# The first batch's expert guessed from v's column sums, and its A formed in two parts, in an attention and mixture-of-experts kernel

## The chip, the cores and the metric

The kernel runs on one core of one Trainium2 chip, in one launch. The metric is the device time of an execution in microseconds (us); before the change the median of 3 runs is 491.9 us (491.01 to 492.18). Short names of the engines: PE multiplies matrices (its weight loads are shown apart, as PEld), DVE, ACT and POOL work element by element, and SP issues most of the DMAs.

## The reference, cut to what matters

Two layers follow each other. The first is a Nystrom attention over 8 batches, 8 heads, 576 tokens and 64 values per head, with 32 landmarks (means over 18 tokens); the second is a sticky mixture of 8 experts over the 512 joined values of a token.

```python
A  = softmax(q @ k_lm.T)      # 576 x 32, one row for each token
Bm = softmax(q_lm @ k_lm.T)   # 32 x 32
C  = softmax(q_lm @ k.T)      # 32 x 576
Z  = Bm.T / (norm_1(Bm) * norm_inf(Bm) + 1e-6)
for _ in range(6):
    Z = 2 * Z - Z @ Bm @ Z
x = A @ Z @ C @ v
...
logits = x @ w_gate
for s in range(S):            # e is sticky along the tokens of a batch
    fresh_e = argmax(logits[b, s])
    e = fresh_e if s == 0 or local_gate[b, s] < 0.5 else prev_e
    out[b, s] = p[e] * (relu(x[b, s] @ w1[e]) @ w2[e])
```

The factors q and k are drawn eight times as large as v; v, w_gate, w1 and w2 are as drawn.

## The kernel before, in words

**One expert for a batch.** All tokens of a batch are sent through one expert, the one that most tokens choose (`votes`, L513). Tokens with another expert are gathered at the end into slots of 128 tokens, one expert and batch to a slot; the code runs one slot always and loops over `whole_slot` for any further ones.

**From attention to the expert.** x is not formed. The chain C, v and the six Newton steps on Z ends in a small matrix `wt` (`newton_w`, L419); `w_w1` (L608) multiplies it with the expert's w1 to G, which is cut into two float32r parts gh and gl; A, transposed, is cut into `ath` and `atl` (`a_split`, L489). `mm1` (L660) multiplies G with A for one chunk of 128 of the 1024 hidden values, with three products (gh with ath, gh with atl, gl with ath); the relu is taken on ACT and DVE (h, hx). The second product (L719, and L713 for the last 64 tokens) multiplies h with w2, also in two parts: wh is cut on ACT (L652), wl is formed on POOL (L657). A batch takes two passes of 8 chunks: first tokens 256 to 575, then tokens 0 to 255 (`PASSES`, L41). So the first pass of a batch needs 320 of its 576 columns of A, and the second pass the rest.

**What sets the order.** The attention of batches 1 to 7 is laid into the expert's chunks of the batches ahead of it: `SECOND` (L1122) and `PLANS` (L1127) hold for each step a time in chunks, at which it is written into the program; `G_AT`, `LATER` and `SLOT_AT` do the same for G, for the later part of the choice and for the slots. Over the first chunks `line_up` keeps all engines to the order as written. The first batch has nothing to hide behind: `first_attention` (L925) writes it by hand, ahead of all chunks. There the votes come last: A, `gate_weights`, `gates` and `votes` give the expert (L527), SP reads it from `regs` (L598), and only then its queue can issue the loads of w1 and w2 (L605, L647), for their address depends on it. `keep_warm` (L157) issues products of zeros, 11 at the start, 8 and 6 later on.

**DMA queues.** SP's queue is in order: an issue that waits holds those behind it. The loads of q and k have two buffers each, of v one.

## Time and profile before

| what | value |
|---|---|
| median of 3 runs | 491.9 us (491.01 to 492.18) |
| the profiled execution | 490.35 us, of which 488.6 us are the profile's span |
| PE busy in the span | 461.4 us (94%) |
| first product of the first chunk (L669) starts | 38.56 us |
| chunk 4 of the first batch starts | 54.56 us |
| second batch's first chunk starts | 103.60 us |
| the slot's expert ends, about | 480 us |
| granted PE clock | half (0.50, 1.2 GHz) from about 23 to 43 us, full (2.4 GHz) otherwise up to the end of the slot |

Times in the rows count from the span's start. A row of a timeline holds the start, the length, the engine, the line, the operation and its tiles (out<-in), and the count of instructions that are merged in it; in square brackets stands how long the engine idled before, and what it waited for. A matmul's length includes its way through the array, so that matmuls overlap: their pitch is the difference of starts.

### The profile page before, as it was taken

The page shows a single profiled execution, that of the slowest core. Times are in us where ns is not written, and L with a number is a line of the kernel's source. Part 1 is how long each engine was busy: PE and PEld are TensorE (multiplying, and loading weights), DVE is VectorE, ACT ScalarE, POOL GpSimd, SP SyncE. Part 2 cuts the span into 40 slices and gives each one's busy share as a digit, 9 for nine tenths or more (in the row PEclk, how much of TensorE's full clock was granted, in tenths as well). Part 3 has the DMA queues.
Part 4 walks back from the last instruction along what each step waited for, and adds up shares of the span by engine and source line. Part 5 has one row for each costly group of instructions (what it writes and reads, how often), then busy time and mean ns, then how long its engine had stood idle before and what let it go on. Part 6 is the DMA issues. An engine that isn't in the chain of part 4 may idle for free. (4 is left out here: it accounts for less than half of the span.)

```text
span 488.6 us, 12068 instructions
## 1 busy us (share of the span) xinstructions
PE 461.4 (94%) x4667; PEld 337.9 (69%) x4669; DVE 269.6 (55%) x807; ACT 210.7 (43%) x554; POOL 234.2 (48%) x355
## 2 busy tenths in 40 slices
...
GB/s 305 394 224 253 26 210 145 283 276 194 8 227 325 232 7 199 358 167 132 257 193 170 61 78 274 153 67 70 259 105 29 152 214 54 48 314 36 64 129 22
DMA packets 38701, 82.01 MB, mean 168 GB/s; under 512 B 3259, under 2 KB 4539, under 8 KB 37872
## 3 DMA queue, kind: packets, MB, share of 16 engines
...
q14 instruction: 23, 0.19, 0.1%
...
## 5 line engine op out<-in xcount | busy, mean ns | idle before, releaser
L719 PE MATMUL py<-wh,h 128*128 128x512 f32 x528 | 170.8, 405 | 1.7 <-ACT h L678 1.0
L657 POOL TENSOR_TENSOR wl<-raw,wh 128x512 fp32r<-128x512 f32 x72 | 92.5, 1303 | 91.2 <-ACT wh L652 80.5
L719 PEld LDWEIGHTS py<-wh,h 128*128 128x128 f32 x528 | 94.0, 188 | 31.1 <-issue 8.7
L678 ACT ACTIVATE h<-ph 128x256 fp32r<-128x256 f32 (+2 forms) x136 | 54.3, 403 | 124.5 <-PE ph L669 105.0
L681 DVE SCALAR_TENSOR_TENSOR h<-ph,h 128x256 fp32r<-128x256 f32 (+1 forms) x136 | 55.3, 409 | 76.7 <-ACT h L678 74.7
L719 PE MATMUL py<-wl,h 128*128 128x512 f32 x264 | 88.7, 394 | 0.0
L669 PE MATMUL ph<-ath,gh 128*128 128x320 f32 (+1 forms) x256 | 79.9, 312 | 1.6 <-DVE hx L684 0.8
L669 PE MATMUL ph<-atl,gh 128*128 128x320 f32 (+1 forms) x256 | 76.5, 299 | 0.0
L669 PE MATMUL ph<-ath,gl 128*128 128x320 f32 (+1 forms) x256 | 76.0, 297 | 0.0
L669 PEld LDWEIGHTS ph<-ath,gh 128*128 128x128 f32 x256 | 48.5, 189 | 17.5 <-issue 6.3
L719 PEld LDWEIGHTS py<-wl,h 128*128 128x128 f32 x264 | 49.5, 188 | 10.7 <-issue 0.5
L669 PEld LDWEIGHTS ph<-atl,gh 128*128 128x128 f32 x256 | 48.7, 190 | 4.1 <-issue 0.5
L669 PEld LDWEIGHTS ph<-ath,gl 128*128 128x128 f32 x256 | 48.6, 190 | 0.5 <-issue 0.5
L652 ACT CAST wh<-raw 128x512 fp32r<-128x512 f32 x72 | 43.1, 631 | 4.0 <-DMA raw<-w 3.9
L640 DVE TENSOR_TENSOR gl<-ph,gh 128x512 fp32r<-128x512 f32 (+1 forms) x19 | 12.5, 662 | 34.8 <-ACT gh L639 34.8
L734 ACT ACTIVATE ys<-py,pall 128x512 f32<-128x512 f32 x32 | 21.0, 689 | 15.6 <-DMA out<-ys 10.1
L639 ACT CAST gh<-ph 128x512 fp32r<-128x512 f32 (+1 forms) x19 | 10.6, 565 | 37.7 <-PE pg L626 26.4
L221 POOL TENSOR_TENSOR t<-q_t 128x288 f32<-128x288 f32 x28 | 21.3, 784 | 5.7 <-DVE regs L527 2.9
L221 POOL TENSOR_TENSOR t<-k_t 128x288 f32<-128x288 f32 x24 | 18.6, 794 | 8.6 <-DMA k_t<-kT 4.1
L713 PE MATMUL pg<-wh,h 128*128 128x512 f32 x56 | 22.4, 400 | 0.0
L713 PE MATMUL pg<-wl,h 128*128 128x512 f32 x56 | 22.3, 398 | 0.0
L626 PE MATMUL ph<-raw,wt 64*32 64x512 f32 (+1 forms) x136 | 19.7, 604 | 2.5 <-DMA raw<-w 2.5
(314 smaller groups left out, 719.8 us busy)
## 6 DMA issues: line engine op xcount, KB each, us to landing
...
raw<-w SPq DMA_DIRECT2D x17, 1024.0 KB, 7.2
v_t<-v SPq DMA_DIRECT2D x8, 1024.0 KB, 6.7
...
q_t<-qT SPq DMA_DIRECT2D x6, 1152.0 KB, 5.7
k_t<-kT SPq DMA_DIRECT2D x6, 1152.0 KB, 9.3
...
```

Of the source, the lines that this page charges most:

```text
L221: add = nc.gpsimd.tensor_add(t9[:, i], src[:, a + i, :, 0:9], src[:, a + i, :, 9:18])
L626: mm = nc.tensor.matmul(ps[g][32 * c:32 * c + 32, 0:n * P], w, w1[r, n * i:n * i + n, a * P:a * P + P], start=True, stop=True)
L639: st["cut"] = nc.scalar.copy(out=gh[:, g, x], in_=ps[g][:, 0:n * P]).ins.name
L640: last = nc.vector.tensor_tensor(out=gl[:, g, x], in0=ps[g][:, 0:n * P], in1=gh[:, g, x].bitcast(F32), op=ALU.subtract)
L652: cut = nc.scalar.copy(out=wh, in_=raw)
L657: nc.gpsimd.tensor_tensor(out=wl, in0=raw, in1=wh.bitcast(F32), op=ALU.subtract)
L669: mm = nc.tensor.matmul(hp, w[:, g, c], x[:, g, s0:s0 + n], start=(i == 0), stop=(i == 5))
L678: nc.scalar.activation(out=h[:, 0:e], in_=hp[:, 0:e], func=AF.Relu)
L681: nc.vector.scalar_tensor_tensor(out=h[:, 384:384 + m], in0=hp[:, 0:m], scalar=0.0, in1=h[:, 0:m].bitcast(F32), op0=ALU.max, op1=ALU.subtract)
L713: nc.tensor.matmul(yps[4], hs[ff][1], w, start=(ff == 0 and w is w2[ff][0]), stop=(ff == NC2 - 1 and w is w2[ff][1]))
L719: nc.tensor.matmul(yps[k], h[:, part + i * P:part + i * P + P], w, start=(f == 0 and part == 0 and w is wh), stop=(f == NC2 - 1 and part = ...
L734: nc.scalar.mul(out=ys, in_=yp, mul=st["pw"][:, k:k + 1])
```

## The change

The first batch's expert is no longer the result of its votes. Four things change in `first_attention`:

1. **A guess.** `guess_sums` sums v over the tokens for each of its 512 columns (20 products of 128-column weights, the upper halves of v as bfloat16, with a column of ones); `guess_scores` multiplies the sums with w_gate (8 products); `guess` takes the largest. The loads of w1 and w2 follow at once (`first_weights`), ahead of v, q and k of later batches on SP's queue. `votes` stops, for the first batch, ahead of its own matmul; tokens that choose another expert than the guessed one would go to the slots, as in any batch.
2. **A in two parts.** `a_scores`, `a_turn`, `a_max0`, `a_exp0`, `a_norm0` and `a_back0` take a part: tokens 256 to 575 ahead of the first chunk, tokens 0 to 255 as steps rs, rm, re, rn and rb among the chunks, at the times of `FIRST`. `gate_weights`, `gates`, the rest of the votes and the choice move there too.
3. **Newton steps with one addition,** for all batches: the two halves of the result are formed by one DVE addition (one of them with a block of zeros) in place of an ACT copy and a DVE addition.
4. **The start's order.** C's scores go ahead of B's, the second half of k of batch 0 comes in two DMAs, the landmarks of batch 1 go behind the first chunks, the fillers are 15 in place of 11, 8 and 6, PSUM banks are named for each use.

The tables `SECOND`, `PLANS`, `G_AT` and `SLOT_AT` have new times, most moved by up to one chunk, some by three; batch 1's second half of w1 and its w2 load at new times (`w1b`, `W2_AT`).

**SP, the loads around the first expert** (q_t, k_t, v_t: q, k, v; `regs`: the chosen expert; raw: w1 and w2; wtd: a store of wt). Before:

```order
L200 DMA q_t<-qT 128x1152
L201 DMA k_t<-kT 128x2x576
L200 DMA q_t<-qT 128x2304
L201 DMA k_t<-kT 128x4x576
L208 DMA v_t<-v 128x4x512
L209 DMA v_t<-v 64x512
L445 DMA wtd<-wt 128x128
L598 TENSOR_LOAD regs
L605 ISA
L605 DMA raw_539<-w 128x2x512
```

Now:

```order
L215 DMA q_t<-qT 128x1152
L217 DMA k_t<-kT 128x2x576
L663 TENSOR_LOAD regs
L670 ISA
L670 DMA raw_377<-w 128x2x512
```

The read of the expert stood behind batch 2's q and k (128x2304), batch 1's v and the store of wt; it now stands right behind batch 1's q and k.

**SP, further on, now** (raw_393 and raw_395 are w2 tiles 4 and 5 of the first batch, raw_572 is tile 6):

```order
L224 DMA v_t<-v 128x4x512
L225 DMA v_t<-v 64x512
L469 DMA wtd<-wt 128x128
L714 ISA
L714 DMA raw_393<-w 128x512
L714 ISA
L714 DMA raw_395<-w 128x512
L215 DMA q_t<-qT 128x2304
L217 DMA k_t<-kT 128x4x576
L714 ISA
L714 DMA raw_572<-w 128x512
```

Batch 1's v, the store of wt and batch 2's q and k stand among the first batch's w2 loads; before, all w2 tiles stood in a row, ahead of the next q.

**PE, the end of the first attention** (L407 Newton steps, L328 C times v, L426 wt, L438 and L506 the gates). Before:

```order
L407 MATMUL ph<-et 32x64 x8
L328 MATMUL py<-v_t,ect 32x64 x20
L407 MATMUL ph<-et 32x64 x8
L328 MATMUL py<-v_t,ect 32x64 x20
L407 MATMUL ph<-et 32x64 x24
L407 MATMUL ph<-et 32x32 x8
L426 MATMUL ph<-et,u 64x32 x8
L438 MATMUL ph<-wg_sb,wt 32x9 x8
L506 MATMUL pg<-at,wgc 32x160 x2
L506 MATMUL pg<-at,wgc 32x128 x2
```

Now, from the first product of the Newton chain (L419) on, with the guess's scores (L550) within, and then the later steps (L431 Newton, L344 C times v, L1048 and L1051 the turning of C):

```order
L419 MATMUL ph<-bt 32x32 x8
L1048 MATMUL one<-ident,ec_293 128x128 x4
L1051 MATMUL one<-ident,ec_293 64x128
L431 MATMUL ph<-et_176 32x64 x8
L550 LDWEIGHTS vs
L550 MATMUL one<-wg_sb,vs 128x8
```

```order
L431 MATMUL ph<-et_177 32x64 x8
L344 MATMUL pg<-v_t,ect 32x64 x8
L431 MATMUL ph<-et_178 32x64 x8
L344 MATMUL pg<-v_t,ect 32x64 x8
L431 MATMUL ph<-et_179 32x64 x8
L1048 MATMUL one<-ident,ec_359 128x128 x4
L1051 MATMUL one<-ident,ec_359 64x128
L431 MATMUL ph<-et_176 32x64 x8
L344 MATMUL pg<-v_t,ect 32x64 x12
L431 MATMUL ph<-et_177 32x32 x8
```

C times v was two blocks between the first three steps; it is now cut into six places, the last four steps have other PE work between them, and the gates are gone from here.

**POOL, around the first chunks** (t: a first sum of landmarks; wl: w2's second part; sa: A). Before:

```order
L657 TENSOR_TENSOR wl<-raw_542,wh 128x512
L657 TENSOR_TENSOR wl<-raw_544,wh 128x512
L221 TENSOR_TENSOR t_908<-k_t 128x288 x2
L657 TENSOR_TENSOR wl<-raw_546,wh 128x512
L657 TENSOR_TENSOR wl<-raw_550,wh 128x512
L657 TENSOR_TENSOR wl<-raw_555,wh 128x512
L221 TENSOR_TENSOR t_948<-q_t 128x288 x2
L657 TENSOR_TENSOR wl<-raw_557,wh 128x512
L657 TENSOR_TENSOR wl<-raw_615,wh 128x512
```

Now:

```order
L240 TENSOR_TENSOR t_592<-q_t 128x288 x2
L724 TENSOR_TENSOR wl<-raw_380,wh 128x512
L724 TENSOR_TENSOR wl<-raw_382,wh 128x512
L240 TENSOR_TENSOR t_662<-q_t 128x288 x2
L724 TENSOR_TENSOR wl<-raw_384,wh 128x512
L724 TENSOR_TENSOR wl<-raw_388,wh 128x512
L724 TENSOR_TENSOR wl<-raw_393,wh 128x512
L724 TENSOR_TENSOR wl<-raw_395,wh 128x512
L1072 TENSOR_TENSOR sa<-sa,mxa 128x2x256
L240 TENSOR_TENSOR t_820<-k_t 128x288 x2
L724 TENSOR_TENSOR wl<-raw_572,wh 128x512
L1087 TENSOR_TENSOR sa<-sa,rsa 128x2x256
```

Two subtractions and scalings of A's rest (128x2x256) stand between the wl now, and the first wl has one t ahead of it.

```diff
@@ -198,7 +213,8 @@
         st["k"] = ld.tile([P, NPAIR, S + M], F32, name="k_t", bufs=2)
         for a in (slice(0, 2), slice(2, 4)) if b < 2 else (slice(0, 4),):
             nc.sync.dma_start(out=st["q"][:, a], in_=qT[b][:, a])
-            nc.sync.dma_start(out=st["k"][:, a, 0:S], in_=kT[b][:, a])
+            for i in (a,) if b or a.start == 0 else (slice(2, 3), slice(3, 4)):
+                nc.sync.dma_start(out=st["k"][:, i, 0:S], in_=kT[b][:, i])
...
     def newton_step(b, st, k, meanwhile=None):
 
-        n0 = 0 if k < 5 else 32
+        n = 64 if k < 5 else 32
         et = st["et"]
         pn = chain(b).tile([P, 2, 64])
-        new = st["et"] = sm.tile([P, 2, 64], F32, name="et", bufs=4)
-        each_place(lambda g, r: nc.tensor.matmul(pn[r, g, n0:64], et[r, g, 0:32], et[r, g, n0:64], start=True, stop=True))
-        if k < 5:
-            nc.scalar.copy(out=new[:, :, 0:32], in_=pn[:, :, 0:32])
+        each_place(lambda g, r: nc.tensor.matmul(pn[r, g, 0:n], et[r, g, 32:64], et[r, g, 0:n], start=True, stop=True))
+        new = st["et"] = next_et()
+        half = lambda t, w: t.rearrange("p g (a x) -> p g a x", x=32)[:, :, 0:(n // 32 - 1) * w + 1:w]
+        nc.vector.tensor_tensor(out=half(new, 1), in0=half(pn, 1), in1=half(et, 2), op=ALU.add)
         if meanwhile:
             meanwhile()
-        nc.vector.tensor_add(new[:, :, 32:64], et[:, :, 32:64], pn[:, :, 32:64])
...
+    def split_part(st, x):
+
+        if "at" not in st:
+            st["at"] = [at.tile([P, 2, S], F32R, name=f"at{p}", bufs=2) for p in "hl"]
+        ah, al = st["at"]
+        nc.scalar.copy(out=ah[:, :, x], in_=st["full"][:, :, x])
+        yield
+        nc.vector.tensor_tensor(out=al[:, :, x], in0=st["full"][:, :, x], in1=ah[:, :, x].bitcast(F32), op=ALU.subtract)
+
+    def guess_sums(st):
+
+        st["pk"] = first_bank[:, 2 * M:3 * M]
+        vb = st["v"].bitcast(BF16).rearrange("p k (f two) -> p k f two", two=2)
+        for a in range(NPAIR):
+            for k in range(NBLK):
+                rows = P if k < 4 else 64
+                nc.tensor.matmul(st["pk"][:, a:a + 1], vb[0:rows, k, P * a:P * a + P, 1], ones[0:rows, 0:1],
+                                 start=(k == 0), stop=(k == NBLK - 1))
+
+    def guess_copy(st):
+
+        st["vs"] = sm.tile([P, NPAIR], BF16, name="vs", bufs=1)
+        nc.scalar.copy(out=st["vs"], in_=st["pk"][:, 0:NPAIR])
+
+    def guess_scores(st):
+
+        w = wg_sb.bitcast(BF16)
+        for h in range(H):
+            nc.tensor.matmul(st["pk"][:, 8:8 + E], st["vs"][:, h // 2:h // 2 + 1].broadcast_to([P, P]), w[:, h, 1:2 * E:2],
+                             start=(h == 0), stop=(h == H - 1))
+        st["vl"] = sm.tile([P, E], F32, name="tot")
+        nc.scalar.copy(out=st["vl"], in_=st["pk"][:, 8:8 + E])
+
+    def guess(st):
+
+        top = sm.tile([P, E], F32, name="top")
+        nc.vector.max(out=top, in_=st["vl"])
+        nc.vector.max_index(out=regs[:, 0, :], in_max=top, in_values=st["vl"])
+
     def gates(st):
 
 
@@ -518,6 +581,8 @@
         nc.vector.reduce_max(out=mx, in_=lg8, axis=AX.X)
         eq = st["eq"] = sm.tile([P, NBLK, E], BF16, name="eq")
         nc.vector.tensor_tensor(out=eq, in0=lg8, in1=mx.unsqueeze(2).broadcast_to([P, NBLK, E]), op=ALU.is_equal)
+        if b == 0:
+            return
...
+            x = slice(128 * g, 128 * g + 128)
+            pt = psa.tile([P, 4, 128], F32, name="one")
+            for k in range(4):
+                nc.tensor.transpose(out=pt[:, k, :], in_=st[f"ec{g}"][:, k * P:k * P + P], identity=ident)
+            nc.scalar.copy(out=st["ect"][:, 0:4, x], in_=pt)
+            pr = psa.tile([P, 512], F32, name="one")[0:64, 0:128]
+            nc.tensor.transpose(out=pr, in_=st[f"ec{g}"][:, 4 * P:S], identity=ident)
+            nc.scalar.copy(out=st["ect"][0:64, 4, x], in_=pr)
+
+        PARTS = (slice(0, 256), slice(0, 8)), (slice(256, S), slice(8, NJ))
+
+        def a_scores(g, p):
+            x = PARTS[p][0]
+            pool, name = (py, "py") if p else (psa, "one")
+            pa[g, p] = pool.tile([P, 512], F32, name=name)[:, 0:x.stop - x.start]
+            for c in range(4):
+                r, a = rows(g, c)
+                nc.tensor.matmul(pa[g, p][32 * c:32 * c + 32, :], st["k"][r, a, S:S + M], st["q"][r, a, x], start=True, stop=True)
+
+        def a_turn(g, p):
+            nc.vector.transpose(out=st["sa"][:, g, PARTS[p][1], :].rearrange("p j l -> p (j l)"), in_=pa[g, p])
+
+        def a_max0(g, p):
+            j = PARTS[p][1]
+            sa, m = st["sa"][:, g, j], mxa[:, g, j]
+            nc.vector.reduce_max(out=m, in_=sa, axis=AX.X)
+            n = 1 if isinstance(g, int) else 2
+            (nc.vector if g == 1 else nc.gpsimd).tensor_tensor(out=sa, in0=sa, in1=m.unsqueeze(2 if n == 1 else 3).broadcast_to(
+                [P, j.stop - j.start, M] if n == 1 else [P, 2, j.stop - j.start, M]), op=ALU.subtract)
+
+        def a_exp0(g, p):
...
+        next(ls["q", 2])
+        b_exp(0)
+        done(ls["q", 2])
+        a_scores(0, 1)
+        c_scores(1)
+        next(ls["k", 2])
+        done(ls["k", 2])
         c_max(0, 0)
-        lms(0, st, "q", 2)
+        b_scores(1)
+        b_exp(1)
         c_max(0, 1)
+        a_scores(1, 1)
+        guess_sums(st)
         c_exp(0)
-        lms(0, st, "k", 2)
-        a_turn(0, 0)
-        b_scores(1)
-        a_turn(0, 1)
-        c_scores(1)
         n = norms(0, st)
         next(n)
         f = newton_first(0, st)
         next(f)
-        a_scores(1)
+        guess_copy(st)
+        c_turn(0)
+        done(n)
+        done(f)
         c_max(1, 0)
+        newton_step(0, st, 0)
+        guess_scores(st)
         c_max(1, 1)
...
-        newton_step(0, st, 0, lambda: (c_sums(st), a_max0(0)))
+        guess(st)
+        newton_step(0, st, 1)
+        first_weights(st)
+        a_turn(0, 1)
+        one.banks = ((pg, "pg"),)
         v = c_v(0, st)
         next(v)
-        a_turn(1, 0)
-        newton_step(0, st, 1)
+        next(v)
+        newton_step(0, st, 2)
+        a_max0(0, 1)
+        next(v)
+        next(v)
+        newton_step(0, st, 3)
+        c_turn(1)
         a_turn(1, 1)
-        a_exp0(0)
+        a_exp0(0, 1)
+        newton_step(0, st, 4)
+        c_sums(st)
+        a_max0(1, 1)
+        next(v)
+        next(v)
+        next(v)
+        newton_step(0, st, 5)
+        a_exp0(1, 1)
+        n0 = a_norm0(0, 1)
+        next(n0)
...
         newton_w(0, st)
-        gate_weights(0, st)
-        a_back0(1)
-        gates(st)
-        split = a_split(0, st)
-        next(split)
-        votes(0, st)
+        done(n0)
+        n1 = a_norm0(1, 1)
+        next(n1)
+        done(n1)
         newton_wt(0, st)
-        nc.gpsimd.dma_start(out=ad[0:P * 2 * NJ].rearrange("(p x) l -> p x l", p=P), in_=st["sa"])
-        keep_warm(6)
+        a_back0(0, 1)
+        a_back0(1, 1)
+        w_w1(st, 0, 2, lambda: done(split_part(st, PARTS[1][0])))
         one.banks = ((psa, "one"),)
-        done(split)
+
+        both = slice(0, 2)
+
+        def scores():
+            for g in range(2):
+                a_scores(g, 0)
+            for g in range(2):
+                a_turn(g, 0)
+
+        def norm():
+            done(a_norm0(both, 0))
+            nc.gpsimd.dma_start(out=ad[0:P * 2 * NJ].rearrange("(p x) l -> p x l", p=P), in_=st["sa"].rearrange("p g j l -> p (g j) l"))
+
+        def back():
+            for g in range(2):
+                a_back0(g, 0)
+            done(split_part(st, PARTS[0][0]))
+
+        st["rest"] = dict(rs=scores, rm=lambda: a_max0(both, 0), re=lambda: a_exp0(both, 0), rn=norm, rb=back)
+
+    def rest():
+        return {k: (lambda k=k: sts[0]["rest"][k]()) for k in ("rs", "rm", "re", "rn", "rb")}
+
+    def first_weights(st):
+
+        e = st["e"] = expert_of(regs[0:1, 0, 0:1].bitcast(I32))
+        st["w1", 0] = load_w1(e, 0, 2)
+        for f in range(3):
+            get_w2(0, f)
+        st["w1", 1] = load_w1(e, 1)
+        get_w2(0, 3)
+        load_v(1, sts[1])
+        for f in range(4, 6):
+            get_w2(0, f)
 
...
-    SECOND = dict(c0=0.1, q2=1.6, k2=1.6, c1=1.6, norms=1.6, a0=2.6, nf=4.1, a1=2.6, t0=4.1, amax=3.1, n0=4.6, t2=4.6,
-        n1=4.1, t4=4.6, aexp=3.6, n2=5.1, cv=6.6, n3=6.6, n4=6.6, anorm=6.6, n5=7.1, nw=7.6, gw=8.1, aback=7.6,
-        gates=8.6, nwt=9.6, votes=8.6, split=10.6, w1=9.6)
+    SECOND = dict(q0=0.1, k0=0.1, c0=0.6, q2=1.6, k2=2.6, c1=3.1, norms=3.1, a0=5.1, nf=6.1, a1=5.6, t0=7.1, amax=6.1,
+        n0=7.1, t2=7.1, n1=6.6, t4=7.1, aexp=7.1, n2=8.1, cv=8.1, n3=7.1, n4=7.6, anorm=8.1, n5=8.1, nw=8.1, gw=8.6,
+        aback=8.1, gates=8.6, nwt=9.6, votes=8.6, split=10.6, w1=10.6, w1b=12.2, fresh=11.6, sticky=13.1, chosen=14.6,
+        own=15.6)
...
-    G_AT = {0: (14, 15), 1: (14, 15), 2: (11, 13), 3: (13, 15), 4: (12, 13), 5: (13, 14), 6: (14, 15), 7: (14, 15)}
-    SLOT_AT = (6.0, 10.5, 7.5, 13.5, 9.0, 15.0, 18.0, 20.5, 27.5, 23.1, 17.5)
-    LATER = ((0.1, 1.0, 6.5, 8.5), (1.6, 1.6, 5.0, 10.5))
+    G_AT = {0: (14, 15), 1: (14, 15), 2: (12, 15), 3: (13, 15), 4: (11, 13), 5: (13, 15), 6: (14, 15), 7: (14, 15)}
+    SLOT_AT = (6.0, 8.0, 7.5, 13.5, 11.0, 17.5, 18.5, 20.0, 28.0, 20.6, 20.5)
+    FIRST = dict(rs=0.6, rm=0.6, re=0.6, rn=1.1, rb=2.6, gw=2.6, gates=3.6, votes=3.6, fresh=4.6, sticky=5.6,
+        chosen=5.6, own=7.1)
+    W2_AT = (12, 12, 13, 13, 15, 15)
     IN_ROW = 9
```

## Rows read from the trace of the kernel before

**Rows 1.** The page: the first line of busy times, one figure for each engine.

```profile
PE 461.4 (94%) x4667; PEld 337.9 (69%) x4669; DVE 269.6 (55%) x807; ACT 210.7 (43%) x554; POOL 234.2 (48%) x355
```

**Rows 2.** Busy times by stretch: length, each engine's busy time, PEclk, DMA share, GB/s.

```profile
0.00:38.56 38.56, 24.56 (x387) 11.21 (x389) 25.83 (x71) 11.45 (x34) 19.22 (x66) 0.80 0.85 306
38.56:54.56 16.00, 14.31 (x111) 8.07 (x104) 11.63 (x35) 11.72 (x42) 14.48 (x16) 0.85 0.49 163
...
103.60:461.10 357.50, 354.70 (x3481) 269.31 (x3480) 195.38 (x588) 155.11 (x391) 167.71 (x231) 1.00 0.46 159
```

**Rows 3.** PE in order of time, first 50 us: start, length, line, tiles.

```profile
15.88 1.47 PE L314 MATMUL one<-ident,ec 128*128 128x128 f32 x10
17.30 0.47 PE L407 MATMUL ph<-et 32*32 32x64 f32 x16
...
25.11 0.44 PE L407 MATMUL ph<-et 32*32 32x32 f32 x16 [0.64 <-DVE et L412]
26.36 0.66 PE L426 MATMUL ph<-et,u 64*64 64x32 f32 x16 [0.81 <-DVE et L412]
...
28.10 1.43 PE L506 MATMUL pg<-at,wgc 128*32 128x160 f32 x16 [0.28 <-DVE wgc L441]
...
35.82 1.11 PE L626 MATMUL ph<-raw,wt 64*32 64x256 f32 x16 [2.53 <-DMA raw<-w]
37.52 1.11 PE L626 MATMUL py<-raw,wt 64*32 64x256 f32 x16 [0.59 <-DMA raw<-w]
38.56 0.63 PE L669 MATMUL ph<-ath,gh 128*128 128x320 f32 x1
...
40.45 2.25 PE L257 MATMUL one<-k_t,ql 64*32 64x288 f32 x16
```

**Rows 4.** The queue of SP in order of time, first 62 us.

```profile
4.11 0.59 SPq L208 DMA_DIRECT2D v_t<-v  x1
...
32.17 0.97 SPq L605 DMA_DIRECT2D raw<-w  x2
```

**Rows 5.** DMA issues of the first 60 us: count, KB each, us to landing.

```profile
q_t<-qT SPq DMA_DIRECT2D x2, 1152.0 KB, 6.0
...
v_t<-v SPq DMA_DIRECT2D x2, 1024.0 KB, 8.1
```

**Rows 6.** DVE in order of time, first 62 us.

```profile
24.97 0.75 DVE L993 TENSOR_REDUCE rsa<-sa 128x18 f32<-128x576 f32 x1
...
27.96 0.77 DVE L1000 STREAM_TRANSPOSE at<-sa 128x576 f32<-128x576 f32 x1
...
31.28 0.16 DVE L527 FIND_INDEX8 regs<-top,tot 128x8 uint32<-128x8 f32 x1
31.36 1.34 DVE L495 TENSOR_TENSOR atl<-at,ath 128x1152 fp32r<-128x1152 f32 x1
...
37.43 0.76 DVE L640 TENSOR_TENSOR gl<-ph,gh 128x256 fp32r<-128x256 f32 x2 [1.25 <-ACT gh L639]
```

**Rows 7.** ACT in order of time, first 62 us.

```profile
27.05 0.34 ACT L430 ACTIVATE wt<-ph 128x64 f32<-128x64 f32 x2 [2.25 <-PE ph L426]
...
39.57 1.65 ACT L652 CAST wh<-raw 128x512 fp32r<-128x512 f32 x3
```

**Rows 8.** POOL in order of time, first 62 us.

```profile
26.37 1.16 POOL L996 TENSOR_TENSOR sa<-sa,rsa 128x576 f32<-128x576 f32 x1 [1.39 <-DVE et L412]
...
31.54 2.45 POOL L221 TENSOR_TENSOR t<-q_t 128x288 f32<-128x288 f32 x2 [2.90 <-DVE regs L527]
...
35.23 1.43 POOL L221 TENSOR_TENSOR t<-q_t 128x288 f32<-128x288 f32 x2
...
44.11 3.74 POOL L657 TENSOR_TENSOR wl<-raw,wh 128x512 fp32r<-128x512 f32 x3
```

**Rows 9.** The granted clock at its fall and its rise, as busy times by stretch.

```profile
22.00:23.00 1.00, 0.42 (x16) 0.26 (x16) 0.97 (x4) 0.21 (x1) 0.81 (x1) 0.89 1.02 382
...
43.00:44.00 1.00, 1.00 (x7) 0.81 (x6) 1.00 (x5) 0.21 (x1) 1.00 (x2) 0.87 0.80 256
```

195 lines of the change are left out of this document (101 added, 94 removed), and 17 rows, old and new, of the table PLANS.

## The prediction

> **What bounds the kernel now.** I read the page's busy times first: PE is busy 94% of the span [rows 1]. The stretches say where it isn't: up to the first chunk PE is busy 24.56 of 38.56 us, and part of that is products of zeros; in the first four chunks 14.31 of 16.00; from the second batch to the slot 354.70 of 357.50 [rows 2]. So 14 us of PE's idle time lie ahead of 38.56, 1.7 in the first chunks, 2.8 in the long middle. A change to the start is worth what it moves the first chunk, less what it puts behind it.
>
> What holds the first chunk is read from PE's order of time [rows 3]. The Newton chain goes from 17.30 to 25.11, then wt's product (26.36), the gates (28.10), the votes; the expert's number is ready on DVE at 31.28 + 0.16 = 31.44 [rows 6]; SP issues w1 at 32.17 [rows 4]; the first product with w1 starts at 35.82, after PE waited 2.53 us for that DMA, the one for its second half at 37.52, the first chunk at 38.56 [rows 3]. wt itself was ready at 27.05 + 0.34 = 27.4 [rows 7]. So w1 comes 8.4 us after wt: that is the wait which the guess takes away. What is late next is wt or A.
>
> **The guess, and when w1 lands.** v is issued at 4.11 and lands some 8.1 us later [rows 4, 5], at 12.2; one more DMA ahead of it costs another 0.5, so 12.7. The sums are 20 products with 128-column weights and one moving column. The trace has none like it: ten turning products with 128-column weights take 1.47 us, 0.147 each [rows 3], so 2.9 at most; below, nothing but the engine's overlap, which I bound with half of that, 1.5. I take 2.5, near the row with equally wide weights: 15.2. In PE's order then follow the first product of the Newton chain (about 0.3), half of the ten turning products (0.75) and step 0 (0.47): 16.7; eight products for the scores at 0.147 are 1.2: 17.9. A copy on ACT, the maximum and its index are about 0.7 (the index alone 0.16): 18.6. From the index to the first issue of w1 it took 32.17 - 31.44 = 0.73, from there to the first product 3.65, and 1.70 more to the second half. That gives 23.0 and 24.7. What the queue still carries then: batch 1's q and k. Batch 0's q, k and v and batch 1's q and k are five loads of 1152 KB, 5.9 MB; at 382 GB/s [rows 9] they are done by about 17, ahead of the issue at 19.3.
>
> **wt.** Before, six pitches from step 0 to wt's product took 26.36 - 17.30 = 9.06, with the last one 1.25 [rows 3]. Step 0 comes at about 16.3, since DVE has no A to turn ahead of the norms; but step 1 stands behind the scores (17.9), and its addition behind the maximum and the index on DVE, so it ends at about 19.1. Four pitches remain to wt's product. With the ACT copy gone, and other PE work laid between the steps, I use 1.25 (bounds: 1.0, that is a step's 0.44 with an addition and two hand-overs, and the mean of before, 1.51): 24.2, and a little for DVE's reductions in between: 24.5. wt follows 27.4 - 26.36 = 1.0 later: 25.5. w1's halves are there (23.0, 24.7), with 2.5 and about 2 us to spare, since the second half is used 1.7 after the first. So the first product with w1 starts at 25.5 in place of 35.82.
>
> **A's first part.** From that product to the first chunk it took 38.56 - 35.82 = 2.74, with A long ready. Now A comes late too. After wt's product DVE still has two reductions over 320 columns with their reciprocals (0.75 x 320/576 = 0.42 each, with two small ones some 0.8) [rows 6], POOL scales twice (1.16 x 320/576 = 0.64 each) [rows 8], DVE turns twice (0.43 each), cuts gl (0.76), and forms atl (1.34 x 640/1152 = 0.74) [rows 6]. Laid end to end from 24.5 with POOL's first scaling beside DVE: A turned at 27.0, gl at 27.8, atl at 28.5. The chunk's first product needs only gh and ath, its second atl. I take 28.3: **a gain of 10.3 us at the first chunk**, of 9 to 11.5 with the bounds of the pitch and of the sums.
>
> One row speaks against it. A pair of POOL's landmark additions took 2.45 us where it began beside DVE's atl (31.36 to 32.70), and 1.43 elsewhere [rows 6, 8]: the two engines did not run side by side. The Trainium skill's "SBUF — State Buffer" (section "SBUF: two separate sides") says that a DVE instruction with two SBUF inputs and a GpSimd instruction take a shared port pair in turn, each for its whole length. By that rule atl can wait for a running addition of POOL, 1.43/2 = 0.7 us, and the time would be 484.6 in place of 483.9. The trace agrees in the size: 1.0 us was lost beside an atl of 1.34. In the sum I leave it at nothing, and in the range at 0.7.
>
> **What is put behind the first chunk.** PE: scores of A's rest, two groups of eight with 256 columns; the 16 products of batch 1's scores took 2.25 us at half clock [rows 3], so 0.9 a group, 1.8. The gates took 1.43 at half clock [rows 3], 0.7 at full; the weights of the gates about 0.3. Together 2.8. The 1.7 us that PE idled in the first four chunks can take some of it; I give back **2.3**. Nothing else of PE's work is new.
>
> DVE gets A's rest (turning, maxima, sums, turning back, cutting: about 4.0 us at 512 of 1152 columns) and the landmarks of batch 1 that stood ahead (about 2.1). In the four chunks of before it was busy 11.63 of 16.00 [rows 2], so 4.4 of these 6.1 fit, and up to 1.7 spill. ACT (11.72 of 16.00) gets 1.2. POOL is full already (14.48 of 16.00): its order now holds a subtraction and a scaling of 512 columns, about 1.0 each, and two more pairs of additions at 1.43. But a wl is used long after it is formed (the wl take 1.25 each [rows 8], eight of them 10, while the second products are spread over all chunks of both passes), so I cost POOL at nothing; if that cover is gone, its 4.9 us are the price.
>
> PE's clock was at half from 22.8 until 43.3, by the shares of the two microseconds in which it changed (0.89 and 0.87) [rows 9]: it rose 4.7 us past the first chunk's start. I let it rise as long after the new start, so it costs what it cost.
>
> **The other edits.** Newton steps without the ACT copy for batches 1 to 7, and the new tables: PE idles 2.8 us in the whole middle [rows 2], so they can hardly gain more than that; moving steps by a chunk can as well lose it. I take nothing, and keep 2.8 to either side. The ten fewer fillers cost nothing, for PE has no other use there.
>
> **The guess's hit.** From the inputs: all 576 tokens of batch 0 choose expert 0, and the scores of the truncated column sums put expert 0 first (4.23, the next 2.49). So the slots stay as they are.
>
> **The sum.** 490.35 (the profiled execution; its span is 488.6) - 10.3 + 2.3 = 482.35. The median of the runs is 1.55 above that execution: **483.9 us**.
>
> **The rivals.**
>
> Better: the first chunk starts at 27 (steps at 1.1, sums at 1.5), DVE's spill is nothing, and the tables win a microsecond of the middle. -11.5 + 2.0 - 1.0: 481.4. For it: PE's free time ahead of the chunk; against: A's chain on DVE, which 28.3 already packs end to end.
>
> The wait comes back in another place, still faster: the sums run at 2.9 and at half clock, v lands at 13.5, or w1's pieces land behind batch 1's q and k; the scores hold step 1 too, so wt and w1 both come 2 us later; DVE's 1.7 spill as well, and the shared port takes 0.7. -8.3 + 2.3 + 1.7 + 0.7: 488.3. For it: ten hand-overs between PE, ACT, DVE and SP stand in a row there, none of them seen in the trace.
>
> **Slower: the seventh w2 tile holds the gates.** In PE's order the gates stand ahead of chunk 4, and they need A's rest, which POOL scales behind the wl of w2's seventh tile; that tile is loaded behind batch 2's q and k (two loads of 1152 KB, about 6 us to landing each [rows 5]), whose buffers come free only when A's rest has its scores. By my reading scores at 31, then 6 to 8 us of q and k: the tile is there at 39 and the gates go at 45, where chunk 4 would start anyway (28.3 + 16 + 1). If that chain takes 8.0 us longer, so that chunk 4 starts past 53.3, the gain is used up; at 55 the kernel is slower, 493.6. For it: the order stands fixed there; against: the tile would have to land at 47 or later, and 382 GB/s of rate would have to halve.
>
> The change doesn't do what it says: the guess misses. Then 576 tokens go through slots, five of 128 in place of none; from 461.1 to 480 is 18.9 us for one: 485 + 5 x 18.9 = 578. Only another rounding on the chip could bring that.
>
> **How the numbers follow.** Forecast 0.53 (own range 482 to 486), better 0.20, the wait in another place 0.19, the gates' chain 0.05 (most of it between 487 and 495), the miss 0.005; the rest for other losses. The range leaves one in ten to each side: 479.8 to 488.9. A measurement of this kernel tells 0.3%, 1.5 us, from no change: above 493.4 is slower, under 490.4 faster. Faster 0.93, the same 0.035, slower 0.035.
>
> **What would show it.** The expert's number at 18 to 20 us and w1's first issue about 0.7 later; PE's first product with w1 at 25 to 26, waiting for wt and not for a DMA; the first chunk at 28 to 29; chunk 4 16.5 to 18.5 us after that; the second batch's first chunk at 95 to 96.5 in place of 103.6; PE's idle time from there on as before. I am wrong if PE waits for raw at the first product, if the gates wait for A while chunk 4 stands behind them, or if the second batch takes another time than before by more than 2 us.

## The result, and the profile after

The changed kernel takes 484.36 us (median of 4 runs, 482.85 to 485.5), the kernel before, timed beside it, 491.51: a ratio of 0.9852, 95% interval 0.9816 to 0.9888. A second set of runs gave 484.21 against 490.75, 0.9868 (0.9841 to 0.9895). So it is faster by 1.3 to 1.5%, and the forecast of 483.9 holds. Its terms do not all hold. The times (us) at which a stage's first chunk starts show it. Each column is one profiled execution; "again" is the changed kernel's second profile, and the last two columns are experiments told below (the one of the old tables is the fastest of its six executions):

| first chunk of | before | changed | again | guess alone | old tables |
|---|---|---|---|---|---|
| first pass | 38.56 | 29.47 | 28.72 | 34.86 | 29.31 |
| its chunk 4 | 54.56 | 49.25 | 47.34 | 50.11 | 47.89 |
| second batch | 103.6 | 102.8 | 101.0 | 98.8 | 101.9 |
| third batch | 166.5 | 160.8 | 158.9 | 161.2 | 164.8 |
| fourth batch | 224.3 | 217.7 | 215.8 | 218.8 | 223.0 |
| span | 488.6 | 483.8 | 481.9 | 483.9 | 490.9 |
| that execution's time | 490.35 | 485.5 | 483.68 | 485.64 | 492.7 |

The first chunk comes 9.1 us earlier (again: 9.8). At the second batch 0.8 (2.6) of that is left, at the third 5.7 (7.5), at the end 4.9 (6.7). So the lead is nearly lost in the first batch and comes back in the second. The windows of the changed kernel show what PE did in between (stretch, its length, busy time and instructions of PE, PEld, DVE, ACT, POOL, then the granted clock, the DMA share and GB/s):

```profile
0.00:29.47 29.47, 23.53 (x358) 12.75 (x358) 19.90 (x62) 9.84 (x33) 13.13 (x62) 0.74 0.88 312
29.47:49.25 19.78, 14.43 (x132) 9.00 (x132) 12.76 (x30) 10.75 (x32) 15.21 (x16) 0.87 0.66 234
49.25:102.80 53.55, 50.38 (x592) 35.43 (x591) 37.81 (x124) 22.60 (x70) 27.27 (x47) 1.00 0.56 193
102.80:456.80 354.00, 351.31 (x3480) 268.13 (x3486) 187.72 (x585) 151.09 (x361) 165.19 (x230) 1.00 0.46 158
```

The kernel before, from chunk 4 to the second batch:

```profile
54.56:103.60 49.04, 47.91 (x562) 34.02 (x563) 30.75 (x101) 20.95 (x63) 21.55 (x35) 1.00 0.53 182
```

Against [rows 2]: ahead of the first chunk PE's idle time fell from 14.00 to 5.94. From the first chunk to the second batch PE idles 5.35 + 3.17 = 8.52 us, before 1.69 + 1.13 = 2.82: **5.7 us are lost there**. PE also works 2.6 us more there (64.81 against 62.22). In the second profile it is 3.5 us of idle time and 3.7 of work, so the split between the two differs from run to run.

Where PE works has moved as well. Two stretches, the first batch's second pass and the second batch, of the kernel before and then of the changed one:

```profile
76.10:103.60 27.50, 27.50 (x270) 19.15 (x267) 15.97 (x57) 14.96 (x41) 9.09 (x18) 1.00 0.55 183
103.60:166.50 62.90, 62.20 (x754) 45.02 (x752) 42.88 (x115) 28.96 (x79) 39.91 (x56) 1.00 0.62 215
```

```profile
69.10:102.80 33.70, 31.48 (x405) 21.93 (x402) 21.31 (x64) 14.22 (x41) 16.16 (x24) 1.00 0.65 219
102.80:160.70 57.90, 57.80 (x723) 42.99 (x722) 39.19 (x112) 26.28 (x66) 34.38 (x53) 1.00 0.62 218
```

The second pass has 405 products in place of 270, mostly moved there out of the first pass, and takes 6.2 us longer. The second batch has 31 fewer and takes 5.0 us less. Over the whole middle the count is the same (3480, before 3481) and PE is busy 3.4 us less (351.31, before 354.70). Of that, 1.1 us are eight turning products that moved ahead of the second batch (they take 8.41 there in place of 9.48); the products with w1 take 13.23 us in place of 16.00 though they are no fewer. That the new places of the steps make this difference fits, but no run isolates it.

PE of the changed kernel, in order of time (start, busy time, line, operation, and in brackets what it waited for):

```profile
13.10 0.25 PE L538 MATMUL one<-ones,v_t 128*128 128x1 bf16 x4 [1.49 <-ACT ec L1038]
13.56 1.10 PE L538 MATMUL one<-ones,v_t 64*128 64x1 bf16 x16 [0.21 <-DMA v_t<-v]
16.22 0.65 PE L431 MATMUL ph<-et 32*32 32x64 f32 x16
16.80 0.37 PE L550 MATMUL one<-wg_sb,vs 128*128 128x8 bf16 x8
25.69 0.32 PE L450 MATMUL ph<-et,u 64*64 64x32 f32 x2 [0.62 <-DVE u L355]
26.65 1.19 PE L693 MATMUL ph<-raw,wt 64*32 64x256 f32 x16 [0.31 <-ACT wt L454]
29.47 0.63 PE L736 MATMUL ph<-ath,gh 128*128 128x320 f32 x1 [0.77 <-ACT ath L527]
38.07 0.39 PE L736 MATMUL ph<-ath,gh 128*128 128x320 f32 x1 [1.25 <-DVE hx L751]
42.46 0.42 PE L736 MATMUL ph<-ath,gh 128*128 128x320 f32 x1 [1.64 <-DVE gl L707]
48.58 0.74 PE L569 MATMUL one<-at,wgc 128*32 128x160 f32 x16 [2.23 <-DVE wgc L465]
86.56 0.19 PE L587 MATMUL one<-eq,ones 128*128 128x40 bf16 x1
93.14 0.61 PE L693 MATMUL ph<-raw,wt 64*32 64x512 f32 x1 [0.49 <-DMA raw<-w]
98.54 0.59 PE L693 MATMUL ph<-raw,wt 64*32 64x512 f32 x1 [1.68 <-DMA raw<-w]
```

The first product with w1 starts at 26.65 and waits for wt, no longer for a DMA (before: at 35.82, behind a wait of 2.53 [rows 3]). Most of the 8.52 us of idle time has names: 1.25, 1.64 and 2.23 in the first four chunks, 0.49 and 1.68 ahead of the second batch. The next rows show the guess (DVE and SP, the first two), and what stands behind the three first waits (ACT and POOL):

```profile
18.07 0.16 DVE L559 FIND_INDEX8 regs<-top,tot 128x8 uint32<-128x8 f32 x1
18.96 0.99 SPq L670 DMA_DIRECT2D raw<-w  x2
35.65 0.62 ACT L719 CAST wh<-raw 128x512 fp32r<-128x512 f32 x1 [2.51 <-DMA raw<-w]
39.36 1.06 POOL L1072 TENSOR_TENSOR sa<-sa,mxa 128x512 f32<-128x512 f32 x1
43.97 1.44 POOL L240 TENSOR_TENSOR t<-k_t 128x288 f32<-128x288 f32 x2 [3.54 <-DMA k_t<-kT]
46.62 1.04 POOL L1087 TENSOR_TENSOR sa<-sa,rsa 128x512 f32<-128x512 f32 x1
```

ACT casts w2's fifth tile ahead of chunk 1's relu and waits 2.51 us for its DMA. POOL forms six low parts (wl) ahead of the subtraction on A's rest, then stands 3.54 us at batch 2's k, and only then scales A's rest; the gates wait for what DVE makes of that. The granted clock (third column from the end; 1.00 is 2.4 GHz, 0.50 is 1.2) fell at 14.0, under the first products behind 1.49 us of idle PE, and rose at 34.5; before it was at half from 22.8 to 43.3 [rows 9]:

```profile
13.00:14.00 1.00, 0.69 (x11) 0.56 (x12) 0.86 (x5) 0.20 (x2) 0.00 (x0) 1.00 0.97 373
14.00:15.00 1.00, 1.00 (x28) 0.88 (x27) 0.30 (x2) 0.16 (x1) 0.00 (x0) 0.50 1.05 396
34.00:35.00 1.00, 1.00 (x10) 0.73 (x13) 1.00 (x5) 0.00 (x0) 1.00 (x2) 0.76 0.72 195
```

### The profile page after: what moved, and what is told of

Its sections match the earlier page's. It is cut to its first block, busy times and chain, and to the rows that moved or that the text cites. A ratio compares the mean times of both kernels' runs of the same rounds, so it can differ in the third digit from the quotient of the medians.

```text
span 483.8 us, 12098 instructions
## 1 busy us (share of the span) xinstructions
PE 459.5 (95%) x4686; PEld 340.5 (70%) x4686; DVE 264.6 (55%) x815; ACT 205.8 (43%) x519; POOL 231.9 (48%) x360
## 5 line engine op out<-in xcount | busy, mean ns | idle before, releaser
L240 POOL TENSOR_TENSOR t<-q_t 128x288 f32<-128x288 f32 x28 | 21.8, 799 | 3.3 <-DMA q_t<-qT 2.7
L240 POOL TENSOR_TENSOR t<-k_t 128x288 f32<-128x288 f32 x24 | 17.5, 748 | 11.7 <-DVE et L434 4.2
L780 PE MATMUL pg<-wl,h 128*128 128x512 f32 x56 | 22.4, 400 | 0.0
L810 POOL TENSOR_TENSOR ys<-ys,yl 64x512 f32<-64x512 f32 x8 | 10.2, 1276 | 22.9 <-ACT yl L808 14.1
```

What stands on the lines that cost most here:

```text
L240: nc.gpsimd.tensor_add(t9[:, i], src[:, a + i, :, 0:9], src[:, a + i, :, 9:18])
L780: nc.tensor.matmul(yps[4], hs[ff][1], w, start=(ff == 0 and w is w2[ff][0]), stop=(ff == NC2 - 1 and w is w2[ff][1]))
L810: nc.gpsimd.tensor_tensor(out=ys[0:64], in0=ys[0:64], in1=yl[0:64], op=ALU.add)
```

## The experiments

Times are medians of 4 to 12 runs in us, with the lowest and the highest; the kernel before stood at 490.4 to 490.8 beside them. A profile shows one execution; where it was the slowest or the fastest of its runs, the text says so.

**The same kernel again.** No edit.

> The changed kernel as it is, for a second profile: its four times lie in two pairs (485.3 and 485.5; 482.9 and 483.4), and the profile that I have is of the slowest. Theory: the pairs differ ahead of the first chunk or in the first four, where waits for DMAs decide (raw tiles, batch 2's k): a profiled execution near 483 shows its first chunk or chunk 4 earlier than 29.47 and 49.25 by about the difference, the stretch from the second batch to the slot again 354.0. Rival: the pairs differ in the middle (PE's waits for w1 ahead of the second batch, 0.49 and 1.68, or a later stretch): the first chunk stays at 29.3 to 29.6 and the middle is shorter by 2.

484.21 (483.68 to 485.09). The theory holds: from chunk 4 on both profiles take the same (434.5 us to the end), and the 1.9 us between them arise ahead of it, 0.75 by the first chunk and the rest in the four chunks behind it. In this profile the clock was at half from 15.6 to 22.4 and from 25.8 to 36.1; the gates waited 0.96, not 2.23.

**The guess alone**, in the kernel before:

```diff
+        guess_sums(st); guess_copy(st); guess_scores(st); guess(st); first_weights(st)   # each at its place
...
+        if b == 0:                  # in votes
+            return
...
-        keep_warm(6)
```

> The kernel before with the guess alone: v's column sums, the scores, the index and w1's and w2's issues from it; A whole, the gates and batch 1's landmarks ahead of the first chunk, old Newton steps and tables. Theory (the guess gives w1 early, and the other half of the gain at the first chunk comes from what was put behind it): the index at 19 to 21, PE no longer waits for raw, the first product with w1 right behind the gates at about 30, the first chunk at 32 to 33.5 (bound by A's cut on DVE), chunk 4 16 us later as before, the time 485.5 to 487. Rival 1: w1 alone is the whole gain and A's rest put behind it only moves the wait: first chunk at 30 or earlier, time 483 to 485. Rival 2: the guess alone gives little, since A and the gates are late anyway: first chunk past 36, time 489.5 or more.

486.42 (485.04 to 488.14; 0.9913, 0.9886 to 0.9939), in the theory's range; the first chunk at 34.86 is later than expected:

```profile
34.86 0.64 PE L701 MATMUL ph<-ath,gh 128*128 128x320 f32 x1 [2.97 <-DVE gl L672]
```

G's low part stood on DVE behind batch 1's landmark sums (32.21 to 34.21). But of the 3.7 us that the first chunk gained, all and one more reach the end (span -4.7), with the old tables and the old order. So w1 from the guess is worth over half of the whole gain: 4.33 us by the medians, of 6.54 and 7.15.

**A's rest ahead on POOL.**

```diff
+            if p == 0:
+                marks["rest less max"] = i_.ins.name   # likewise "rest scaled"
...
+        if after:
+            not_ahead_of(low, after)   # low: wl; tiles 4, 5 after "rest less max", 6, 7 after "rest scaled"
...
+                    not_ahead_of(add, "rest scaled")   # batch 2's additions
```

> The changed kernel, with POOL's order turned in two places: the subtraction of A's rest ahead of the low parts of w2's fifth and sixth tile, the scaling of A's rest ahead of batch 2's k additions and of the seventh tile. Theory (the wait of the gates for A's rest costs 2 to 4 us in the first four chunks): the subtraction at 37 in place of 39.4, the scaling at 40 to 42 in place of 46.6, chunk 4 at 46 to 47 in place of 49.25, and the time 481.5 to 482.5 if the second batch takes the lead over. Rival 1: the time is absorbed by the choice of batch 1's expert and its w1: chunk 4 earlier by as much, but PE waits longer for raw ahead of the second batch (2.2 us now, then 4 to 5), and the time stays at 484 to 485. Rival 2: the wait moves to the sixth tile's low part: chunk 4 stays at 49, time 484 to 485.5.

485.02 (484.31 to 486.76): no gain. POOL subtracts at 36.79 and scales at 41.08, as expected, but chunk 4 starts at 50.27. The outcome is rival 2's, the place is another than it named. PE now waits 2.76 us ahead of chunk 3, for G's low parts, which stand on DVE behind A's rest being turned back, and 0.76 at the gates:

```profile
43.56 0.63 PE L740 MATMUL ph<-ath,gh 128*128 128x320 f32 x1 [2.76 <-DVE gl L709]
45.28 2.50 POOL L726 TENSOR_TENSOR wl<-raw,wh 128x512 fp32r<-128x512 f32 x2
45.41 2.93 DVE L531 TENSOR_TENSOR atl<-at,ath 128x512 fp32r<-128x512 f32 x1 [1.31 <-ACT ath L529]
49.60 0.74 PE L571 MATMUL one<-at,wgc 128*32 128x160 f32 x16 [0.76 <-DVE wgc L467]
```

ACT had waited 2.60 for the seventh tile ahead of ath; then atl took 2.93 us beside two low parts on POOL (0.99 in the changed kernel), and the gates' weights stood behind it. The clock was at half once more, from 43.2 to 46.7.

**The old tables** of batches 2 to 7, the G products and the slot, in the changed kernel.

```diff
-        2: (-13.4, -10.9, -10.4, -11.9, ...
+        2: (-12.9, -10.9, -10.4, -11.4, ...
```

> The changed kernel with the old tables of batches 2 to 7, of the G products and of the slot (those of the first two batches stay new). Theory (PE idles 2.7 to 2.8 us in the whole middle with either): within 1 us of the changed kernel, 483.4 to 485.4, the middle's idle time 2 to 4 us. Rival: the new tables are what holds the lead of 5 us from the third batch to the end: 487 or more, with PE's idle time in the middle up by 3 or more.

496.71 (492.7 to 499.21): slower than the kernel before (1.0125, 1.0092 to 1.0158). The rival holds, and far beyond the 487 that it gave. PE's longest waits in the second and the third batch (what waits, for whom, us in total, times, longest; the first stands at 167.8, in the third):

```profile
PE ph L736 <- ACT bm L318: 1.9, 1, 1.9
PE one L431 <- DVE et L434: 1.6, 1, 1.6
PE py L786 <- ACT wh L719: 1.3, 1, 1.3
```

PE idles 3.3 us in the second batch, in the changed kernel 0.1. The profile is of the fastest execution, so some 4 us of the median's loss stand in no trace. With the new Newton step and A in two parts, the tables, costed at nothing, are needed for the gain.

**Fillers against the clock's fall.**

```diff
         a_scores(1, 1)
+        fill(6)
         guess_sums(st)
...
         newton_step(0, st, 1)
+        fill(2)
...
+        fill(1)
         newton_w(0, st)
```

> The changed kernel with nine more products of zeros on PE (384 columns each): six between A's second scores and v's sums, where PE stood idle from 11.61 to 13.10, two behind Newton step 1 (idle 0.53), one ahead of wt's product (idle 0.62). Its clock fell to half at 14.0 and stayed there through the whole Newton chain; in the kernel before it fell at 22.8, in the guess alone at about 26. Theory (the fall follows the idle stretch and costs 2 us: steps of 0.65 in place of 0.45, two turnings of 1.5 in place of 0.8): the clock full past 20, wt's product at 23.3 to 24.5 in place of 25.69, the first chunk at 27 to 28.4, the time 482 to 483.2. Rival 1 (the clock falls all the same): no step earlier, 484 to 485. Rival 2 (wt comes earlier, but A's chain on DVE and POOL sets the first chunk): wt at 24, the first chunk at 28.8 or later, 483.5 to 485.

483.59 (482.32 to 485.89): not told from the changed kernel. The mechanism is close to what the theory has: up to the first chunk the clock is at half only from 17.4 to 20.8, wt's product at 24.16, the first chunk at 27.82. In this profile, the slowest of the six executions, what was won is lost two chunks later:

```profile
36.43 0.62 ACT L719 CAST wh<-raw 128x512 fp32r<-128x512 f32 x1 [3.62 <-DMA raw<-w]
38.84 0.60 PE L736 MATMUL ph<-ath,gh 128*128 128x320 f32 x1 [4.04 <-DVE hx L751]
```

The fifth tile is issued when the first low part frees one of four raw buffers (30.22) and is cast 6.2 us later; relu stands behind its cast. PE idles, and the clock is at half again from 37.8 to 44.7, and once more from 99.3 to 102.7, ahead of the second batch at 104.1. While the tile is on its way the loads run as fast as at the start, where they run without a pause (396 to 402 GB/s from 14 to 18):

```profile
34.00:36.00 2.00, 0.81 (x12) 0.00 (x0) 0.84 (x2) 0.00 (x0) 1.29 (x2) 1.00 1.05 387
36.00:38.00 2.00, 0.00 (x0) 0.00 (x0) 0.00 (x0) 1.57 (x5) 0.87 (x1) 0.96 0.96 397
```

So the tile may be late by the four buffers or by the bytes ahead of it; no run separates the two.

**The gates' way cleared.**

```diff
+                not_ahead_of(lq, "tile 7")        # batch 2's q and k behind w2's last tiles
...
+        not_ahead_of(atl, ("wgc", 0))             # on DVE: both gl, turning back, gates' weights, atl
```

POOL's order is that of the run with A's rest ahead.

> The changed kernel with the whole way of the gates cleared: POOL's two steps on A's rest ahead as in the run with the rest ahead, batch 2's q and k issued behind w2's seventh and eighth tile, batch 2's k additions behind their low parts, on DVE both low parts of the second G, the turning back and the gates' weights ahead of atl. Theory (the wait went on to the seventh tile's DMA, to atl that took 2.93 us beside two wl, and to the gates' weights behind it): chunk 3 at 41.5 to 42.5, chunk 4 at 45.5 to 47.2 in place of 49.25 and 50.3, time 481.3 to 483. Rival 1 (absorbed later, by w1 of batch 1, whose choice comes no earlier): chunk 4 as expected, PE's wait for raw ahead of the second batch up from 2.2 to 4 or more, time 484 to 485. Rival 2 (batch 2's q and k now come late): PE or DVE waits for q_t or k_t past 50, chunk 8 at 69 or later, time 484 or more.

484.59 (482.53 to 485.6). The gates wait for nothing any more, and chunk 4 stands 17.9 us behind the first chunk in place of 19.8 and 18.6, though at 47.82, since the first chunk came at 29.94. The next four chunks then take 21.3 in place of 19.8: cleared in one place, given back in the next. That is not rival 1's place, for the waits for raw ahead of the second batch stay at 2.3. It is nearer to rival 2 (chunk 8 at 69.08), but PE waits there for C's exponentials (0.57) and the choice's scan (1.02), not for q or k.

**G's low part first**, in the guess alone.

```diff
-    for half in halves:
-        next(half)
     w_w1(sts[0], 0, 2)
```

> The guess alone, with G's low part on DVE ahead of batch 1's landmark sums, ahead of which PE waited 2.97 us (first chunk at 34.86). Theory (there the early start is carried whole to the end): the first chunk at 32 to 33, the time 2 us below that of the guess alone, 483.8 to 485.2. Rival: batch 1's landmarks, now late, hold its scores in the first chunks, the gain is given back: 486 to 487.

488.63 (12 runs, 485.02 to 491.2; 0.9963, 0.994 to 0.9986): slower than without the edit, though barely clear of it, and a miss for the theory. The wait in question did fall, from 2.97 to 1.14. But its profile had the first chunk at 35.98, since the whole chain came 3 us later. The code up to there is the same, but the clock was at half from 17.6 to 24.4 (and again from 27.8 to 34.6, 38.0 to 41.5 and 58.5 to 61.9), in the guess alone only from 26.1 to 39.8. The turning products of the two, the guess alone ahead:

```profile
17.47 1.52 PE L314 MATMUL one<-ident,ec 128*128 128x128 f32 x10
```

```profile
18.32 2.44 PE L314 MATMUL one<-ident,ec 128*128 128x128 f32 x10
```

That explains the profile, not all of the 2.2 us between the medians: landmarks that come late may cost the rest (PE waits 0.79 ahead of batch 1's scores at 37.9, and 1.51 ahead of the last block's products at 58.7); this stays open.

**The old Newton step with the old tables.**

```diff
+        if b:
+            if k < 5:
+                nc.scalar.copy(out=new[:, :, 32:64], in_=pn[:, :, 32:64])
+            nc.vector.tensor_add(new[:, :, 0:32], et[:, :, 0:32], pn[:, :, 0:32])
+            return
...                                          # and the tables of the run with the old tables
```

> The changed kernel with the old tables, and for batches 1 to 7 the old Newton step as well (ACT copies one half, DVE adds the other), so that only the first attention and the first two batches' tables are new. The old tables alone gave 492.7 to 499.2, PE waiting in the second batch for a Newton step (1.65), for wh (1.27) and for a relu (1.92). Theory (the old tables are fitted to the old step's length on DVE and ACT): waits gone, 484 to 487. Rival (they are fitted to where batch 1's steps stood in the old first passes): the time stays at 491 or more, with waits of over 3 us in the second batch.

490.16 (487.76 to 492.72): between the changed kernel and the old tables, and no faster than the kernel before (0.9991, 0.997 to 1.0011). So it misses the theory's 484 to 487. The longest waits of the second and the third batch are down to 0.28, 0.29 and 0.55, as the theory has it, which is worth 6.5 us against the old tables. More than half of what is left sits in the first batch, where the steps' places (new) meet the old step: a wait of 1.36 for one at 68.73, 2.52 for w1 at 100.40, the second batch only at 106.5. From there on it takes 2.7 us more than the changed kernel. This run has the guess and A in two parts, yet it is 3.7 us slower than the guess alone: A in two parts pays only with step, places and tables that fit it.

**Relu first.**

```diff
+        not_ahead_of(cut, ("relu", 1))     # the casts of tiles 4 and 5 behind chunk 1's relu
...
+                not_ahead_of(cut, "wh5")   # G's second cut behind both casts
```

> The changed kernel with chunk 1's relu on ACT ahead of the casts of w2's fifth and sixth tile. The fifth tile is issued only when the first low part has freed one of four raw buffers (31.87 in the changed kernel), and ACT waited 2.51 us for it with the relu behind; with the fillers, where the first chunk came 1.65 us earlier, that wait was 3.62 and PE stood 4.04 us ahead of chunk 2. Theory (ACT's order passes the tile's wait on to chunk 2): chunk 2 at 7.2 to 8.0 us after the first chunk in place of 8.6, no wait there over 0.4, and 0.6 to 1.2 us off the end, 483 to 483.8. Rival (the wait goes on to chunk 3, whose G waits behind A's rest and batch 1's scores on ACT and DVE): chunk 2 earlier, chunk 4 as before (18.6 to 19.8 after the first chunk), 484 to 484.8.

484.89 (482.56 to 489.63). The wait ahead of chunk 2 is 0.39 in place of 1.25, so ACT's order was its cause. On the time the rival is near (484 to 484.8). Where a usual run loses it, this profile can't tell, for it is of the slowest execution (489.63): PE waits 2.09 ahead of chunk 3, and chunk 4 comes 21.8 us after the first. POOL's scaling came ahead there (41.91), and the gates waited 4.20: for the seventh tile's DMA (ACT 4.07), an atl of 2.55 beside two low parts, and the weights behind it.

**The second half of w1 ahead of w2.**

```diff
-... w1b=12.2, ...
+... w1b=10.65, ...
```

> The changed kernel with the second half of batch 1's w1 issued right behind the first, ahead of w2's first four tiles. PE waited for that DMA 1.68 and 1.46 us in the two profiles, just ahead of the second batch. Theory: the second wait gone (under 0.4), the first one as it was or a little longer (0.5 to 1.2), the second batch 1 to 1.6 us earlier and the end with it: 482.6 to 483.4. Rival (w2's tiles, now late, hold the second batch's first second products): a wait for wh or wl between 103 and 112, time 484 to 485.

485.48 (484.12 to 487.98). PE's wait of 1.68 for w1 is gone, and in its place stands 1.97 at 98.59 for a relu behind a cast that waits 2.48 for its w2 tile. That is the rival in kind, only earlier than it said (103 to 112). One load's place in the queue was bought with another's.

**All together** (the fillers, the gates' way, relus first, w1's half).

> All together: the fillers, the gates' way cleared as in that run, relus of the chunks 0 to 2 ahead of the casts of w2's tiles 3 to 7, and the second half of batch 1's w1 ahead of w2. Theory (what the change lost is three waits behind the first chunk, and each can be taken away): first chunk at 27 to 28, chunk 4 at 43 to 45.5, second batch at 96.5 to 99, time 478.5 to 481. Rival 1 (batch 1's own chain, not PE, sets the second batch: its choice comes no earlier): chunk 4 as early as that, but PE waits 3 us or more for w1 ahead of the second batch, time 482 to 484. Rival 2 (the DMA queue is the bound: tiles 4 to 7 and batch 2's q and k land no earlier): waits for raw or k_t of 2 us or more between 34 and 55, time 482 to 484.

486.09 (482.95 to 487.18): a miss, no better than any one, and above both rivals' times. In this profile, of the slowest execution, the clock was at half only from 17.1 to 20.5 at the start, as with the fillers alone. Chunk 4 came at 46.88, but the second batch at 104.3; PE waited 1.53 for the choice's scan at 57.05 and 2.25 ahead of the second batch (0.42 for w1, 1.83 for a relu), and the clock was at half again from 41.0 to 44.4, from 58.1 to 61.5 and from 99.0 to 102.5.

**The votes earlier.**

```diff
+                            if apart and s0 == 0 and f == 1:
+                                not_ahead_of(mm, ("votes", 1))
```

> The changed kernel with the product of batch 1's votes moved ahead on PE: in the second profile of the changed kernel eq was ready at 80.34, but the votes stood behind 18 second products, at 84.69, so w1 was issued some 4 us late and PE waited 0.76 and 1.46 us for it ahead of the second batch. Here they stand behind six of them and one chunk. Theory (that place on PE is the cause of both waits): the votes 2.5 to 3.5 us after the gates in place of 6.0, both waits for raw gone or under 0.4, the second batch 31.5 to 32.3 us after the second pass's first chunk in place of 33.7 to 33.9, the time 482 to 483. Rival 1 (w1 and w2 are bound by the DMA queue, not by the issue): the issue 3 us earlier, the waits for raw together still over 1.5, 484 to 485. Rival 2: the waits are gone, but PE waits as long for wh or wl of w2 behind it, as when the second half of w1 came ahead of w2: 483.5 to 485.

484.01 (483.49 to 486.42). The theory on the place holds in full: the votes at 81.05, both waits for raw gone, the second batch 31.2 us behind the second pass, 3.0 earlier than in the second profile. And yet the end is where it was, not at 482 to 483. At 182 both stand level. Of the 3 us, 1.75 are lost up to the third batch and 1.46 right behind its start, where PE waits for DVE:

```profile
160.35 0.62 ACT L719 CAST wh<-raw 128x512 fp32r<-128x512 f32 x1 [3.43 <-DMA raw<-w]
162.04 0.39 PE L736 MATMUL ph<-ath,gh 128*128 128x320 f32 x1 [1.50 <-DVE mx L310]
```

Batch 2's expert came no earlier with it, 137.81 against 136.91 in the second profile. One reading is that the tables spread the next batch's attention over DVE, ACT and POOL, so that PE, 3 us ahead, meets it 3 us too early; that is argued, for no run moved the tables along with the lead. None of the versions tried beats the changed kernel by more than its runs differ (the lowest median is 483.59, with the fillers).

## Why the prediction was right, and where not

The number was right; of the working, the first half was, and two errors in the second half cancel. By the signs that the prediction itself set, it was wrong in two of three: the gates wait for A's rest with chunk 4 behind them (2.23 us), and the second batch takes 57.9 us in place of 62.9.

- **The guess.** Index 18.07 + 0.16 (predicted 18.6), first issue 18.96 (19.3), w1 never waited for: right. v's last part was there only at 13.56 (12.7), but the sums took about 1.6 us (2.5 taken, 1.5 the lower bound), the eight scores 0.37 (1.2). All of this is for these inputs, where the guess hits; no run shows a miss. (The last rival's sum comes to 579.5, not 578.)
- **wt and the first chunk.** The first product with w1 at 26.65 (predicted 25.5), bound by wt as said; the first chunk at 29.47 and 28.72 (28.3). The steps' pitch was mis-sized: step 2 starts at 19.14, as laid out, but the four pitches from there to wt's product are 1.64 each, in place of 1.25 and beyond the bound of 1.51. Between them stand C's second turning and C times v (in four places by the trace), and I left the clock's fall where it was, at 22.8. It came at 14.0, so that a step took 0.65 and a turning 1.3. "The ten fewer fillers cost nothing" belongs here: with nine fillers more the clock was at half for 3.4 us only, and the chunk came at 27.82.
- **A's order.** ath, not atl, released the first product, and atl took 0.83 (0.74 estimated): right.
- **The give-back of 2.3: the term that failed.** It measured 8.3 us, and 7.2 in the second profile. The added work was near (2.6 and 3.7, estimated 2.8), but I counted on 1.7 us of PE's idle time to take some of it up; 5.7 more (3.5) came instead. The prediction costed POOL at nothing, and A's rest stands there in front of the gates; the rival of the seventh tile described this chain. Its bound held: chunk 4 at 49.25 is short of 53.3. But the chain does not set the time, for with POOL's order turned, and with the gates' wait gone altogether, the time stayed (485.02, 484.59). What holds the first batch as a whole is not shown.
- **The second batch** was expected at 95 to 96.5 and came at 102.8 and 101.0. I took for granted that the first batch runs as fast as before once it starts. But batch 1's expert is chosen at 87.31 and 85.44, before at 86.42, in the guess alone at 81.64: it did not come earlier with the first chunk. Its votes stand on PE behind second products; with the votes moved up, the second batch came at 98.0, and the end stayed.
- **Tables and Newton at 0, to 2.8 either way: wrong in the other direction.** From the second batch to the end it takes 381.0 in place of 385.0, and the second batch alone is 5.0 shorter. PE's idle time in the middle stayed as it was (2.69, before 2.80), so the bound on waiting was kept. What I had left out is that PE can be busy less with as many products: 3.4 us, of which 1.1 are work that moved ahead. Without the new tables the same change is a loss.
- **The sum.** Measured: 490.35 - 9.1 + 8.3 - 4.0 = 485.5, in the second profile 490.35 - 9.8 + 7.2 - 4.1 = 483.7. Predicted before the step to the median: -10.3 + 2.3 + 0, which is 482.35. Two errors of opposite sign, of 5 to 6 and of 4 us, cancel: that is luck. The 1.55 added for the median is luck too. It came from three runs, and in the later sets the kernel before has its median at most 0.4 above that execution; the changed kernel's profiled execution was the slowest of its four and 1.1 above their median. Without the 1.55 the forecast is 2 us low.
- **Shared port.** No row of before had A's low part beside POOL's low parts. They show it now: atl took 2.93, 2.55 and 2.13 us, and each time ended 0.55 to 0.57 us after the second of two low parts that POOL had in a row. In the changed kernel it took 0.99, and POOL's pair of additions beside it 1.90 in place of 1.44. This agrees with the Trainium skill's "SBUF — State Buffer" (section "SBUF: two separate sides"), by which a DVE instruction with two SBUF inputs and a GpSimd instruction that reads SBUF take turns. At the first chunk, which I weighed, it cost at most 0.1 (atl 0.83 for 0.74).
